# Key loads of the second and third group moved ahead of weight loads in a delta-rule and two-layer feed-forward kernel

## The chip, the cores and the metric

The kernel runs on one core of a Trainium2 chip. The metric is the device time of one execution in microseconds, as the median of several runs.

## What is computed

The reference runs a delta-rule attention over 768 steps and puts two feed-forward layers behind it. All is in fp32. Batch 4, 8 heads, head size 48, so 3072 tokens of width 384; both layers go from 384 to 2048 and back.

```python
k_n = k / (norm(k) + 1e-6)
for t in range(S):
    y[:, :, t] = einsum('bhd,bhde->bhe', q[:, :, t], state)
    v_old = einsum('bhde,bhd->bhe', state, k_n[t])
    state = state + beta[t] * einsum('bhd,bhe->bhde', k_n[t], v[t] - v_old)
x = y as 3072 x 384
h = x @ w_in;   g = h if h >= 1, 0 if h <= -1, else (h + 1)**2 / 4;   x = g @ w_out
h = x @ w_in2;  g = max(h, 0)**2;                                     out = g @ w_out2
```

## The kernel before

The 768 steps are cut into 24 chunks of 32 steps. Four chunks form a group (six groups). For each chunk TensorE makes the products of its keys and queries (`gram`, line 319; for the first group line 354). The dependence between steps inside a chunk needs the inverse of a triangular matrix, and that is done for a whole group at once (`tri`: a transpose on VectorE, small operations for the norms, then 30 pairs of multiply and add, lines 478 and 479, and a transpose back, line 482). The first group's inversion runs on VectorE in two halves that `ld` and `dld` join on TensorE (lines 506 and 514); the inversions of the other groups run on GpSimd. After it each chunk takes its four steps in order, because the state passes from chunk to chunk: ks and yy (line 542), tr (556), sps (591) with its yy (579), and xt (623), the transposes that bring the result into layout for the feed-forward layer.

The first layer then works on blocks of four chunks, 512 tokens. A block has 16 units, one for each 128 columns of the hidden width. Unit f makes hidden product f (nine matmuls into h, 128 x 512, three of them with the low half of x), ScalarE and VectorE make g of it and split it into a high and a low half, and TensorE adds out product f - 2 (nine matmuls into three accumulators `acc`). Each unit has two slots, 2f and 2f + 1, into which other work is put by hand: `put_a` and `put` add a piece at a slot number. In block 0 these are the grams of the third group, the chunk steps of the second group, and the inversion of the third group. In block n are the chunk steps of group n + 1.

Weights arrive as raw halves of 0.39 MB (`load_w`), two to a weight tile, in the order `needed`. Block 0 is also where they are unpacked: two sign-bit passes on ScalarE (`whole_bits`, lines 195 and 196), joined words on VectorE (`make`, line 202), the high half on ScalarE (`upper`, line 232) and the low half on VectorE (`lower`, line 236). Tiles 0 to 2 are made during the first group's chain of steps, the others in units 0 to 12 (`between`): unit f takes up the raw halves of tile f + 3.

All loads go out on SyncE's queue, which takes them in program order. `loads(m, ...)` lets at most m of the loads it lists be under way (`pace`). Keys for a gram come into the ring `kqg` of KG = 2 buffers (`load_kg`), so that a third chunk waits for the gram of the first. Keys for the chunk steps (`load_kq`) and values (`load_kv`) have rings of their own. A few early arrays stand in weight tiles that come into use only later: `spare` and `room`.

On TensorE the order is that of the program. Its first products are the grams of the first two groups, then the first group's chain, then block 0.

Of the kernel before, what the change touches and what calls it, by code (L numbers as in the profile page):

```python
# [8 lines left out]
F32 = mybir.dt.float32  # L9
# [16 lines left out]
def kernel(  # L26
# [23 lines left out]
    NCH, P, DM = out.shape  # L50
    NF = w1.shape[0]
    B, H, T = 4, 8, 32
    D = DM // H
    KT = DM // P
    B2 = B // 2
# [12 lines left out]
    KQ, KG = 3, 2  # L68
# [6 lines left out]
    ring = ctx.enter_context(tc.tile_pool(name="ring", bufs=1))  # L75
# [16 lines left out]
    def weights(x):  # L92
        if x not in both:
            both[x] = wp.tile([P, 2, 2, DM], F32R, tag=f"w{x}", name=f"w{x}")
        return both[x]
# [23 lines left out]
    kqt, kvt, gp, nt, xh, xl = {}, {}, {}, {}, {}, {}  # L119
# [17 lines left out]
    kqg = {}  # L137

    def load_kg(c):
        if c < NCH and c not in kqg:  # L140
            kqg[c] = fetch_kq(c, ring.tile([P, B2, H, 2 * T], F32, tag="kqg", bufs=KG, name="kqt"))

    def fetch_kq(c, t):
        both = [nc.sync.dma_start(
            t[64 * o:64 * o + D].rearrange("p b h x -> p (b h x)"), kq[c, D * o:D * (o + 1)]
        ).ins for o in range(2)]
        pace(*both)
        return t
# [12 lines left out]
    def pace(*ins):  # L161

        m = flight[0]
        if m:
            if len(sent) >= m:
                for x in ins:
                    wait_for(x, sent[-m], "few loads under way")
            sent.append(ins[-1])
# [31 lines left out]
    def joined_words(raw, shape):  # L200
        t = ring.tile(shape, F32, tag="wl", bufs=WL, name="wl")
        nc.vector.scalar_tensor_tensor(
            t.bitcast(I32), raw[..., 1], 3, raw[..., 0],
            ALU.logical_shift_left, ALU.bitwise_or,
        )
        return t
# [14 lines left out]
    def halves(x):  # L221
        return sign_bits(raws[x])

    def whole_bits(x):
        for f in halves(x):
            f()

    def make(x):
        words[x] = joined_words(raws.pop(x), [P, 2, DM])

    def upper(x):
        nc.scalar.copy(weights(x)[:, :, 0], words[x])

    def lower(x):
        t = weights(x)
        nc.vector.tensor_sub(t[:, :, 1], words.pop(x), t[:, :, 0].bitcast(F32))
# [55 lines left out]
    def value(c):  # L292

        g, j = group_of[c]
        return nc.gpsimd.tensor_mul(
            kvt[c][:, 1], kvt[c][:, 1],
            nt[g][:, j * H:(j + 1) * H].rearrange("p (h o) -> p h o", o=1)
            .to_broadcast([P, H, D]),
        )
# [6 lines left out]
    def gram(c, lo=0, hi=2, late=0, eng=None, side=0):  # L306


        n, j = group_of[c]
        if j == 0 and lo == 0:  # L310
            gp[n] = ring.tile([P, 2, GC, H, T], F32, tag="gp", bufs=2, name="gp")
            if GROUPS[n] < GC:
                nc.gpsimd.memset(gp[n][:, 0, GROUPS[n]:], 0.0)
        g = att([P, H, hi - lo, T], "g", side)
        src = kqg[c]

        def one_(b, h, p, pd):
            x = src[pd, b // 2, h]
            nc.tensor.matmul(  # L319
                g[p, h].rearrange("p x i -> p (x i)"), x[:, 0:T], x[:, lo * T:hi * T],  # L320
                start=h == 0, stop=True, skip_group_check=True,
            )

        per_bh(one_)
        kqg.pop(c)
        if late < 2:
            load_kg(c + KG)

        dst = gp[n][:, lo:hi, j].rearrange("p x h i -> p h x i")
        if late > 1:  # L330
            nc.scalar.copy(dst, g)

        def keep():
            (eng or nc.vector).tensor_mul(
                dst,
                dst if late > 1 else g,
                mask[:, lo:hi].rearrange("p (o x) i -> p o x i", o=1)
                .to_broadcast([P, H, hi - lo, T]),
            )

        if late:
            return keep
        keep()
# [22 lines left out]
    def mask_of_head(c):  # L366
# [5 lines left out]
    spare = {  # L372
        "z": (NF - 1, 0), "d": (NF - 1, 1024), "l": (NF - 2, 0), "cross": (NF - 2, 1024),
        "kq": (NF - 3, 0), "u0": (NF - 3, 1024),
    }
    rooms = {}

    def room(name, size):
        x, lo = spare[name]
        if x not in rooms:  # L380
            rooms[x] = wp.tile([P, 4 * DM], F32, tag=f"w{x}", name="room")
        return rooms[x][:, lo:lo + size]
# [398 lines left out]
    NW, NP = 2 * NF, NF  # L781
# [26 lines left out]
    def put(n, slot, *fs):  # L808
        for i, f in enumerate(fs):
            exb.setdefault(SL * n + slot + i, []).append(f)  # L810
# [9 lines left out]
    def put_a(n, slot, *fs):  # L820
        exa.setdefault(SL * n + slot, []).extend(fs)

    def two_grams(c):
        gram(c)
        gram(c + 1, side=1)
# [26 lines left out]
    with tc.manual_schedule():  # L852
# [22 lines left out]
        def loads(m, what):  # L875
            flight[0] = m
            for kind, c in what:
                kind(c)
            flight[0] = 0

        def ws(a, z):
            return [(load_w, needed[x]) for x in range(a, z)]

        def kgs(c):
            return [(load_kg, c)]

        def kvs(c):
            return [(load_kv, c)]

        loads(2, kgs(4) + kgs(5) + ws(0, 1) + kgs(6) + ws(1, 2) + kgs(7) + kvs(0) + ws(2, 3) + kvs(1) + ws(3, 4))  # L890
        loads(1, kvs(2) + ws(4, 5) + kvs(3) + ws(5, 9))
        begin, pre, steps, end = tri(0, V, True)
        begin()
        pre[0]()
# [3 lines left out]
        for c in range(FIRST_GROUP):  # L898
            save0(c)
        masks.append(gram(6, late=2, eng=G))  # L900
        whole_bits(0)
        masks.append(gram(7, late=2, eng=G))
        ins = go(steps)
        rows0()
# [10 lines left out]
        begin1, pre1, steps1, end1 = tri(1, G)  # L915
# [2 lines left out]
                chunk_steps(c) for c in range(FIRST_GROUP)]  # L918
        ld0(0)
        ld0(1)  # L920
        make(0)
        dld0(0)
        dld0(1)
        upper(0)
        s0()
        t0()
        lower(0)
        ld0(2)
        s1()
        ld0(3)  # L930
        t1()
        whole_bits(1)
        begin1()
        k0()
        pre1[0]()
        k1()
        make(1)
        dld0(2)
        go(pre1[1:-2])
        s2()  # L940
        q1()
        t2()
        upper(1)
        go(pre1[-2:])
# [22 lines left out]
        x3()  # L967
        x0()
        k3()
        loads(2, ws(9, 12) + [(load_kq, 4)] + ws(12, 13) + [(load_kq, 5)] + ws(13, 16) + kgs(8) + ws(16, 18) + kgs(9))  # L970
        loads(2, ws(18, NW))
        turn[0] = None

        put(0, 12, end1)
        put(0, 11, lambda: value(4))
        put(0, 12, lambda: value(5))
        put(0, 14, lambda: value(6))
        put(0, 21, lambda: value(7))
        for c, at_ in ((4, (13, 15, 17, 18)), (5, (19, 20, 21, 22)),
                       (6, (23, 24, 25, 26)), (7, (27, 28, 29, 30))):  # L980
            def steps_of(c=c, box={}):
                if c not in box:
                    box[c] = chunk_steps(c)
                return box[c]
            for i, slot in enumerate(at_):
                put_a(0, slot, lambda i=i, g=steps_of: g()[i]())
        put(0, SL - 1, lambda: first2(RAW))

        at, ready = {}, {}
        for c, slot in ((8, 8), (10, 10)):  # L990
            ready[c + 1] = slot
            put_a(0, slot, lambda c=c: two_grams(c))
        for n in range(2, NB):
            todo = []
            for j, c in enumerate(range(FIRST[n], FIRST[n] + SIZES[n])):
                if n < NB - 1 and 2 * j < SIZES[n + 1]:
                    x = FIRST[n + 1] + 2 * j
# [3 lines left out]
            for i, (mark, s_) in enumerate(todo):  # L1001
                slot = SL * (n - 1) + i * SL // len(todo)
# [95 lines left out]
```

## Time and profile before

| | us |
|---|---|
| median of 3 runs (lowest to highest) | 1055.08 (1054.01 to 1056.84) |
| the profiled execution | 1058.46 |
| its span, first to last instruction | 1056.7 |
| TensorE busy | 988.0 (93%) |
| VectorE / ScalarE / GpSimd busy | 518.2 / 433.9 / 297.1 |
| mean granted TensorE clock, of full speed | 0.976 |

How to read it: the span is cut into stretches, and for each the profile has the busy time of every engine, the clock that TensorE was granted, as a share of full speed, and what the DMA engines moved. Full speed is 2.4 GHz, the lower level 1.2 GHz; a share in between means that both levels occur in the stretch. TensorE's idle time is then put down to what ended it. SyncE has no work of its own; its rows are the moments at which loads are sent. A load lands some us later, and the chain of waits shows from when to when.

### The profile page before, as it was taken

The page shows a single profiled execution, that of the slowest core. Times are in us where ns is not written, and L with a number is a line of the kernel's source. Part 1 is how long each engine was busy: PE and PEld are TensorE (multiplying, and loading weights), DVE is VectorE, ACT ScalarE, POOL GpSimd, SP SyncE. Part 2 cuts the span into 40 slices and gives each one's busy share as a digit, 9 for nine tenths or more (in the row PEclk, how much of TensorE's full clock was granted, in tenths as well). Part 3 has the DMA queues.
Part 4 walks back from the last instruction along what each step waited for, and adds up shares of the span by engine and source line. Part 5 has one row for each costly group of instructions (what it writes and reads, how often), then busy time and mean ns, then how long its engine had stood idle before and what let it go on. Part 6 is the DMA issues. An engine that isn't in the chain of part 4 may idle for free.

```text
span 1056.7 us, 29989 instructions
## 1 busy us (share of the span) xinstructions
PE 988.0 (93%) x13416; PEld 838.0 (79%) x13416; DVE 518.2 (49%) x801; ACT 433.9 (41%) x745; POOL 297.1 (28%) x414
## 2 busy tenths in 40 slices
PE   5787387899999999999999999999999999999998
PEld 4675266678888777888888888998989999999997
DVE  4437246657555655765544666544333343333333
ACT  2237135435544453554554554333323333333322
POOL 1478005922950780395110112111020020100000
PEclk9998678899999999999999999999999999999999
DMA  6437731144334434334333114101010000000000
GB/s 139 140 91 210 210 75 33 49 135 108 99 117 135 120 101 115 98 87 150 107 100 99 60 60 128 37 1 60 1 53 8 1 30 1 1 30 1 31 1 30
DMA packets 33937, 80.68 MB, mean 76 GB/s; under 512 B 4368, under 2 KB 11664, under 8 KB 33808
## 3 DMA queue, kind: packets, MB, share of 16 engines
q1 hardware_dynamic: 33808, 78.76, 25.5%
q8 instruction: 105, 1.72, 0.7%
q14 instruction: 24, 0.20, 0.1%
HBM read 63.01 MB, written 15.73 MB: 75 GB/s over the span
## 4 chain that ended last, share of the span: by engine, by line
PE 82%; DMA 8%; DVE 5%; ACT 2%; issue 2%; SPq 0%; POOL 0%; ACTq 0%; DVEq 0%; POOLq 0%
PE h L638 35%; PE acc L638 35%; DMA raw<-in_w_dram 4%; DMA kqt<-in_kq_dram 2%; PE tr L556 2%; PE yy L579 2%; PE sps L591 2%; PE yy L542 2%; PE ks L542 1%; DVE gp L482 1%; PE g L319 1%; PE xt L623 1%; DMA room<-in_kq_dram 1%; DVE gm L418 1%; ACT r L670 1%
## 5 line engine op out<-in xcount | busy, mean ns | idle before, releaser
L638 PE MATMUL acc<-w,gg 128*128 128x384 f32 x1152 | 217.3, 337 | 1.7 <-ACT e L697 1.7
L638 PE MATMUL h<-x2s,w 128*128 128x512 f32 x864 | 214.6, 392 | 0.0
L638 PEld LDWEIGHTS acc<-w,gg 128*128 128x128 f32 x1152 | 203.9, 187 | 10.0 <-ACT e L697 2.3
L638 PEld LDWEIGHTS h<-x2s,w 128*128 128x128 f32 x864 | 160.8, 188 | 29.3
L638 PE MATMUL h<-xh,w 128*128 128x512 f32 x576 | 155.1, 405 | 4.8 <-ACT r L670 4.8
L638 PE MATMUL acc<-gh,w 128*128 128x512 f32 x576 | 157.3, 409 | 0.8 <-ACT gh L687 0.8
L678 DVE TENSOR_TENSOR rg<-rg 128x512 f32<-128x512 f32 x96 | 69.6, 725 | 143.4 <-ACT rg L677 143.4
L638 PEld LDWEIGHTS h<-xh,w 128*128 128x128 f32 x576 | 107.8, 192 | 29.4 <-ACT r L670 5.3
L638 PEld LDWEIGHTS acc<-gh,w 128*128 128x128 f32 x576 | 105.9, 192 | 24.6 <-ACT gh L687 1.2
L677 ACT ACTIVATE rg<-h,zero 128x512 f32<-128x512 f32 x96 | 66.2, 689 | 138.4 <-PE h L638 138.4
L689 DVE TENSOR_TENSOR gg<-rg,gg 128x512 fp32r<-128x512 f32 x96 | 67.2, 700 | 104.0 <-ACT gg L687 104.0
L670 ACT ACTIVATE r<-h,one 128x512 f32<-128x512 f32 x96 | 66.0, 687 | 124.1 <-PE h L638 123.6
L687 ACT CAST gg<-rg 128x512 fp32r<-128x512 f32 x96 | 59.7, 622 | 118.3 <-PE acc L638 114.2
L687 ACT CAST gh<-g 128x512 fp32r<-128x512 f32 x96 | 59.5, 620 | 117.5 <-DVE g L674 72.3
L689 DVE TENSOR_TENSOR gl<-g,gh 128x512 fp32r<-128x512 f32 x96 | 74.7, 778 | 62.0 <-ACT gh L687 43.1
L479 POOL TENSOR_TENSOR tx<-tx,t 128x30 f32<-128x30 f32 (+9 forms) x150 | 100.7, 671 | 11.5
L671 DVE TENSOR_SCALAR g<-r 128x512 f32<-128x512 f32 x96 | 47.7, 497 | 112.0 <-ACT r L670 111.5
L478 POOL TENSOR_TENSOR t<-tx,gm 128x30 f32<-128x30 f32 (+9 forms) x150 | 93.3, 622 | 13.4 <-DVE tx L457 2.2
L674 DVE SCALAR_TENSOR_TENSOR g<-r,g 128x512 f32<-128x512 f32 x96 | 76.7, 799 | 35.2 <-ACT g L673 35.2
L638 PE MATMUL acc<-gl,w 128*128 128x512 f32 x288 | 83.3, 398 | 0.0
L638 PE MATMUL h<-xl,w 128*128 128x512 f32 x288 | 83.0, 397 | 0.1
L673 ACT ACTIVATE g<-g 128x512 f32<-128x512 f32 x96 | 60.4, 629 | 33.1 <-DVE g L671 31.6
(117 smaller groups left out, 902.1 us busy)
## 6 DMA issues: line engine op xcount, KB each, us to landing
raw<-in_w_dram SPq DMA_DIRECT2D x64, 384.0 KB, 3.5
kqt<-in_kq_dram SPq DMA_DIRECT2D x86, 192.0 KB, 4.0
kv<-in_kv_dram SPq DMA_DIRECT2D x24, 384.0 KB, 3.5
w2f<-wl SPq DMA_DIRECT2D x32, 192.0 KB, 3.9
w2r<-w2f SPq DMA_DIRECT2D x16, 384.0 KB, 3.1
x<-e SPq DMA_DIRECT2D x18, 256.0 KB, 2.3
x2r<-x SPq DMA_DIRECT2D x6, 768.0 KB, 4.9
out_dram<-e SPq DMA_DIRECT2D x23, 192.0 KB, 2.0
```

The lines of the kernel that those rows point to most:

```text
L478: eng.tensor_mul(t, by.to_broadcast(shape), of.to_broadcast(shape))
L479: return eng.tensor_add(rest, rest, t)
L542: per_bh(lambda b, h, p, pd: nc.tensor.matmul(o[p, h], kqt[c][pd, b // 2, h, x * T:(x + 1) * T], st[pd, b // 2, h], start=h == 0, stop=x = ...
L638: nc.tensor.matmul(o, *((r, l) if swap else (l, r)), **flags)
L670: marks[0] = nc.scalar.activation(r, h, AF.Relu, bias=one)
L671: marks[1] = nc.vector.tensor_scalar(g, r, 2.0, 0.5, ALU.min, ALU.mult)
L673: nc.scalar.activation(g, g, AF.Square)
L674: nc.vector.scalar_tensor_tensor(g, r, -1.0, g, ALU.add, ALU.max)
L677: marks[0] = nc.scalar.activation(r, h, AF.Relu, bias=zero)
L678: marks[1] = nc.vector.tensor_mul(g, r, r)
L687: nc.scalar.copy(ghi, g)
L689: nc.vector.tensor_sub(glo, g, ghi.bitcast(F32))
```

## The change

- Key chunks 6 and 7 of the second group no longer go through the ring `kqg`: they have places of their own in weight tiles 12 and 11 (`spare`), so that all four of the group's loads are sent one behind the other, ahead of any weight.
- During the first group's chain 14 raw weight halves are loaded, the last ten of them one at a time, in place of nine, the last five one at a time.
- After the chain come four halves, the keys of chunks 4 and 5 for their steps, the keys of chunks 8 and 9 for their grams, and four more halves. The last ten halves are sent from slot 9, behind the keys of chunks 10 and 11, which the grams of 8 and 9 ask for.
- Unpacking of tiles 0 and 1 stands later among the chain's steps.
- Slots: the end of the second group's inversion 12 to 11; steps of chunks 4, 5 and 6 one to three slots earlier; the grams of chunks 10 and 11 from slot 10 to 11.

```diff
     def load_kg(c):
         if c < NCH and c not in kqg:
-            kqg[c] = fetch_kq(c, ring.tile([P, B2, H, 2 * T], F32, tag="kqg", bufs=KG, name="kqt"))
+            if f"kg{c}" in spare:
+                t = room(f"kg{c}", B2 * H * 2 * T).rearrange("p (b h x) -> p b h x", b=B2, h=H)
+            else:
+                t = ring.tile([P, B2, H, 2 * T], F32, tag="kqg", bufs=KG, name="kqt")
+            kqg[c] = fetch_kq(c, t)
...
         "kq": (NF - 3, 0), "u0": (NF - 3, 1024),
+        "kg6": (NF - 4, 0), "kg7": (NF - 5, 0),
     }
...
-        loads(2, kgs(4) + kgs(5) + ws(0, 1) + kgs(6) + ws(1, 2) + kgs(7) + kvs(0) + ws(2, 3) + kvs(1) + ws(3, 4))
-        loads(1, kvs(2) + ws(4, 5) + kvs(3) + ws(5, 9))
+        loads(2, [(load_kg, c) for c in range(4, 8)] + kvs(0) + kvs(1) + ws(0, 4))
+        loads(1, kvs(2) + kvs(3) + ws(4, 14))
...
         masks.append(gram(6, late=2, eng=G))
-        whole_bits(0)
         masks.append(gram(7, late=2, eng=G))
...
         ld0(1)
-        make(0)
         dld0(0)
         dld0(1)
-        upper(0)
+        whole_bits(0)
         s0()
         t0()
-        lower(0)
+        make(0)
         ld0(2)
         s1()
+        upper(0)
         ld0(3)
         t1()
+        lower(0)
...
         k1()
-        make(1)
         dld0(2)
         go(pre1[1:-2])
         s2()
         q1()
+        make(1)
         t2()
...
-        loads(2, ws(9, 12) + [(load_kq, 4)] + ws(12, 13) + [(load_kq, 5)] + ws(13, 16) + kgs(8) + ws(16, 18) + kgs(9))
-        loads(2, ws(18, NW))
+        loads(2, ws(14, 18) + [(load_kq, 4), (load_kq, 5)] + kgs(8) + kgs(9) + ws(18, 22))
...
-        put(0, 12, end1)
+        put(0, 9, lambda: loads(2, ws(22, NW)))
+        put(0, 11, end1)
...
-        for c, at_ in ((4, (13, 15, 17, 18)), (5, (19, 20, 21, 22)),
-                       (6, (23, 24, 25, 26)), (7, (27, 28, 29, 30))):
+        for c, at_ in ((4, (12, 13, 14, 15)), (5, (17, 18, 19, 20)),
+                       (6, (22, 23, 24, 25)), (7, (27, 28, 29, 30))):
...
-        for c, slot in ((8, 8), (10, 10)):
+        for c, slot in ((8, 8), (10, 11)):
```

SyncE's queue from the end of the chain's weight loads to the third group's keys, before. `raw` is a weight half, `kqt` half of a chunk's keys (two loads for a chunk), `kv` a chunk's keys and values in token layout; the first `kqt` row is chunk 6, the next ones are 4, 5, 8, 9, and the last row begins with 10 and 11.

```order
L186 DMA raw<-in_w_dram 128x768 x4
L144 DMA kqt<-in_kq_dram 48x1024 x2
L155 DMA kv<-in_kv_dram 128x768 x3
L186 DMA raw<-in_w_dram 128x768 x3
L144 DMA kqt<-in_kq_dram 48x1024 x2
L186 DMA raw<-in_w_dram 128x768
L144 DMA kqt<-in_kq_dram 48x1024 x2
L186 DMA raw<-in_w_dram 128x768 x3
L144 DMA kqt<-in_kq_dram 48x1024 x2
L186 DMA raw<-in_w_dram 128x768 x2
L144 DMA kqt<-in_kq_dram 48x1024 x2
L186 DMA raw<-in_w_dram 128x768 x14
```

The same stretch after: the row of eight holds chunks 4, 5, 8 and 9, the row of four chunks 10 and 11.

```order
L190 DMA raw<-in_w_dram 128x768 x10
L148 DMA kqt<-in_kq_dram 48x1024 x2
L159 DMA kv<-in_kv_dram 128x768 x3
L190 DMA raw<-in_w_dram 128x768 x4
L148 DMA kqt<-in_kq_dram 48x1024 x8
L190 DMA raw<-in_w_dram 128x768 x4
L148 DMA kqt<-in_kq_dram 48x1024 x4
L190 DMA raw<-in_w_dram 128x768 x10
```

The keys of chunks 10 and 11 stood behind the 14 last halves; now ten halves stand behind the keys.

TensorE in block 0, before: unit 5's hidden product, the grams of chunks 10 and 11 (one row of 64), out product 3, hidden product 6.

```order
L638 MATMUL h<-xl,w_1696 128x512 x3
L319 MATMUL g<-kqt 32x64 x64
L638 MATMUL acc_1708<-gh,w_1696 128x512 x2
L638 MATMUL acc_1709<-gh,w_1696 128x512 x2
L638 MATMUL acc_1710<-gh,w_1696 128x512 x2
L638 MATMUL acc_1708<-gl,w_1696 128x512
L638 MATMUL acc_1709<-gl,w_1696 128x512
L638 MATMUL acc_1710<-gl,w_1696 128x512
L638 MATMUL h<-xh,w_1735 128x512 x6
```

After, from the same hidden product on:

```order
L643 MATMUL h<-xl,w_1681 128x512 x3
L643 MATMUL acc_1693<-gh,w_1681 128x512 x2
L643 MATMUL acc_1694<-gh,w_1681 128x512 x2
L643 MATMUL acc_1695<-gh,w_1681 128x512 x2
L643 MATMUL acc_1693<-gl,w_1681 128x512
L643 MATMUL acc_1694<-gl,w_1681 128x512
L643 MATMUL acc_1695<-gl,w_1681 128x512
L323 MATMUL g<-kqt 32x64 x64
L643 MATMUL h<-xh,w_1720 128x512 x6
L643 MATMUL h<-xl,w_1720 128x512 x3
L547 MATMUL ks<-st,kqt 32x48 x32
L547 MATMUL yy<-st,kqt 32x48 x32
```

Out product 3 goes ahead of the two grams, and ks and yy of chunk 4 stand right behind hidden product 6.

## Rows read from the trace of the kernel before

**Rows 1.** Stretches: length; busy (instructions) per engine; clock; DMA share; GB/s

```profile
97.90:143.40 45.50, 21.70 (x293) 17.00 (x294) 13.99 (x18) 11.32 (x17) 5.23 (x7) 0.62 0.69 190
143.40:221.70 78.30, 67.96 (x1473) 53.14 (x1471) 50.28 (x70) 42.06 (x69) 45.25 (x65) 0.91 0.15 40
221.70:400.00 178.30, 177.76 (x3658) 143.13 (x3658) 108.91 (x173) 86.49 (x161) 89.00 (x132) 1.00 0.42 121
400.00:1056.70 656.70, 650.38 (x5691) 564.80 (x5689) 298.57 (x450) 258.66 (x436) 104.08 (x120) 1.00 0.16 51
```

**Rows 2.** The chain of waits from 79 us: start, length, what

```profile
79.36 4.99 DMA raw<-in_w_dram
...
102.32 4.05 DMA kqt<-in_kq_dram
...
130.11 5.80 DMA kqt<-in_kq_dram
...
183.50 2.29 PE h L638 x9
```

**Rows 3.** Timeline of SyncE's queue: start, first to last issue, what, count

```profile
37.58 0.33 SPq L155 DMA_DIRECT2D kv<-in_kv_dram  x1
...
47.87 10.82 SPq L186 DMA_DIRECT2D raw<-in_w_dram  x4
...
104.97 24.62 SPq L186 DMA_DIRECT2D raw<-in_w_dram  x14
129.63 20.34 SPq L144 DMA_DIRECT2D kqt<-in_kq_dram  x10
```

**Rows 4.** Timeline of TensorE in block 0: start, length, what [idle before, releaser]

```profile
97.86 2.93 PE L638 MATMUL h<-xh,w 128*128 128x512 f32 x6 [4.41 <-ACT r L670]
...
105.73 0.42 PE L319 MATMUL g<-kqt 48*32 48x64 f32 x2 [2.58 <-DMA kqt<-in_kq_dram]
...
108.27 2.93 PE L638 MATMUL acc<-gh,w 128*128 128x512 f32 x6
...
112.27 1.64 PE L638 MATMUL h<-xh,w 128*128 128x512 f32 x6
...
135.26 0.39 PE L319 MATMUL g<-kqt 48*32 48x64 f32 x2 [20.66 <-DMA kqt<-in_kq_dram]
...
143.36 1.53 PE L638 MATMUL h<-xh,w 128*128 128x512 f32 x6
```

**Rows 5.** TensorE's waits from 143.36 to 221.72 (total, times, longest); next block's start

```profile
PE yy L542 <- DVE xl L626: 6.5, 3, 2.5
PE xt L623 <- ACT kv L607: 2.7, 1, 2.7
...
221.72 1.67 PE L638 MATMUL h<-xh,w 128*128 128x512 f32 x6
```

**Rows 6.** Timeline in the first group's chain: VectorE, TensorE twice, ScalarE

```profile
28.63 1.05 DVE L502 STREAM_TRANSPOSE room<-tx 128x512 f32<-128x512 f32 x1
...
33.11 1.90 PE L506 MATMUL z<-room 32*32 32x16 f32 x128
...
40.43 0.93 PE L556 MATMUL tr<-kv,gp 32*32 32x48 f32 x34 [1.46 <-issue]
...
64.73 0.91 ACT L195 ACTIVATE raw<-raw 128x768 f32<-128x768 f32 x1
```

**Rows 7.** Timeline around the third group's inversion on GpSimd: VectorE and GpSimd

```profile
148.98 0.95 DVE L236 TENSOR_TENSOR w<-wl,w 128x768 fp32r<-128x768 f32 x1
...
168.12 1.28 POOL L448 TENSOR_TENSOR gm<-gm,st 128x256 f32<-128x256 f32 x1 [64.75 <-DVE st L437]
...
181.98 1.58 DVE L236 TENSOR_TENSOR w<-wl,w 128x768 fp32r<-128x768 f32 x1
...
216.51 0.62 POOL L479 TENSOR_TENSOR tx<-tx,t 128x30 f32<-128x30 f32 x1
...
225.23 2.18 DVE L482 STREAM_TRANSPOSE gp<-tx 128x1024 f32<-128x1024 f32 x1
```

## The prediction

> **What bounds the kernel now.** I read the 40 slices first, then the table by stretch, then the chain of waits and the timelines of SyncE and TensorE in the stretch that stood out. From 221.7 us on TensorE is busy in 177.76 of 178.30 us and then in 650.38 of 656.70 us, at a granted clock of 1.00 [rows 1]. That part is a block of TensorE work, the change leaves its matmuls alone, and it moves as a whole: whatever is won or lost must happen before the second block of layer one starts its first product at 221.72 [rows 5]. Before that, two stretches are poor. In 97.9 to 143.4 TensorE is busy 21.70 of 45.50 us at a clock of 0.62; in 143.4 to 221.7 it is busy 67.96 of 78.30 at 0.91 [rows 1].
>
> The first is a wait for a load. The chain that ended last runs through DMAs from 79.36 to 135.91 [rows 2], and TensorE stands still for 20.66 us before the scores (the key products, "grams") of chunk 10, with the keys named as releaser [rows 4]. Behind that gram, in program order, stand out product 3 and hidden product 6, so all of block 0 waits. Why the keys are late is seen on SyncE's queue: after 104.97 it sends 14 weight halves, 24.62 us of them, and only at 129.63 the keys of chunk 10 [rows 3]. None of those 14 halves was what TensorE needed next; the weights of unit 5 had been there. The second stretch has another cause: waits of 6.5 us for VectorE's xl (three yy products share a PSUM buffer with the transposes just ahead of them) and of 2.7 us for ScalarE [rows 5], most of its 10.34 idle us.
>
> **The change, part by part.**
>
> A. Key chunks 6 and 7 get places in weight tiles 12 and 11. Before, gram 7 stood on TensorE in front of the first inverse product (z, line 506), which began at 33.11 although its last input, VectorE's transpose, was done at 28.63 + 1.05 = 29.68 [rows 6]. With all four key chunks under way first, gram 7 ends before that, and z can start 3.4 us earlier. What follows, up to the chain's end at 79.36 [rows 2], is a chain of short dependent products, so it should shift as a whole. Against it: ten weight halves (before, five) are now loaded beside the chain, one at a time. TensorE has gaps there in which it waits for nothing the profile shows, 1.46 us at 40.43 where loads run [rows 6]. In the chain's second half, which before had hardly any load beside it, I allow for three such gaps of some 1 us. So A is between 0 and 3.4; I take **2.5 us**, since at most part of the gaps can grow. The moved conversions (make, upper and lower of tile 0 and 1) go behind chain work on VectorE and ScalarE, so they cost the chain nothing; their cover is that the first hidden product comes 40 us later.
>
> B. From the end of the chain to hidden product 6. Before, 79.36 to 143.36, 64.0 us. After, step by step from the chain's end. Hidden 4 starts when ScalarE has let go of the buffer h, not when a load lands [rows 4]: 97.86 - 79.36 = 18.5 us, unchanged. From its start to the end of the two grams 8 and 9 it was 108.27 - 97.86 = 10.4, of which 2.6 was a wait for keys [rows 4]: 7.8 without it, so 26.3. Out 2 took 112.27 - 108.27 = 4.0, at half clock [rows 4]: 30.3. Hidden 5, nine matmuls at full clock, 2.29 us as at 183.50 [rows 2]: 32.6. Grams 10 and 11 and out 3 took 143.36 - 135.26 = 8.1 at half clock [rows 4], half of that at full clock, 4.1: hidden 6 at 36.7 to 40.7. I take **39**, against 64.0: a gain of **25 us**.
>
> That needs the keys in time. Load rate: between 79.36 and 106.37 thirteen loads landed (nine weight halves, four key chunks; the queue below the diff counts them), 2.08 us each [rows 2]; the fourteen halves after it took 1.76 each [rows 3]. After the change eight loads bring the keys of 9: 16.6 us. In front of them may still lie what the queue held back: the one-at-a-time loads are 3.5 us apart [rows 3]; if they begin at about 37, as before at 37.58 [rows 3], the twelve end at about 79, as late as the chain, and the keys of chunk 6 and two of three value loads (the queue rows below the diff) stand behind them, some 6 us. So keys 9 land 17 to 23 us after the chain's end and gram 9 wants them at about 24. Keys 10 go out when gram 8 has ended and four more halves have been issued, 21 to 27, and land 4 to 6 us later (before: 5.8 [rows 2]), 25 to 33, against a need at 35 (hidden 5's end and out 3). It fits with a margin of 2 us at the late end. If both are late, B loses up to 5: its range is 20 to 27. The ten halves that now stand behind keys 10 and 11 on SyncE's queue go out from 27 on, 1.76 each, all there by 46; the last is asked for in unit 12, after 75. That is free.
>
> The Trainium skill (DMA: Bandwidth & Descriptors, Anatomy of one DMA) prices a single DMA at about 2.0 us plus its bytes over 436 GB/s, for these 0.39 MB an estimate of 2.9 us; the rows above say 3.5. By the page the twelve loads would end at about 72 and rival 1 would be less likely; by the rows they end with the chain. I go by the rows.
>
> C. From hidden 6 to the first product of the next block: 221.72 - 143.36 = 78.4 us. The slots of chunks 5 to 7 now leave half a unit or more between a transpose and the yy product that shares its buffer, so the 6.5 us go, and the 2.7 us at least in part. In their place chunks 4 and 6 now have only one product of 2.3 us between ks and tr, where VectorE must subtract in between: perhaps 1 us for each. VectorE is still loaded by the start of the third group's inversion in units 7 to 9. If nothing were idle it would be 68 us at the same clock. I take **70**, a gain of **8**, with 1 (the stalls only change their name) and 11 (no idle, full clock) as ends.
>
> D. What is late next: the inversion of group 3 on GpSimd. It ran from 168.12 to 217.1, 49 us, and VectorE's transpose of its result began at 225.23 [rows 7], 8 us later. Its start is tied to unit 9, its end to a slot in unit 16; those come some 14 us nearer to each other. So VectorE will wait about 5 us for GpSimd there; TensorE has some 12 us of products (hidden 16 and 17, a pair of grams, two outs, ks) ahead of the first tr that needs the result. I take a cost of **1 us**, 0 to 4.
>
> The sum: 2.5 + 25 + 8 - 1 = **34.5 us**. Against the profiled execution (1058.46 us, span 1056.7) that is 1024; the runs' median, 1055.08, lies 3.4 us below the profiled one, and taken off the median it gives 1020.6, so **1021 us**. The ends add up to 17 and 41.4; both sets of ends at once are unlikely.
>
> **The rivals.**
>
> 1. The keys of 8 to 11 are still late, since the one-at-a-time loads run past the chain and hold back everything behind them. For it: the estimate above ends at the same moment as the chain. Against: only 8 loads are then left before keys 9, not 13. Price: about 8 us of wait in place of the 20.66. Time 1029.
>
> 2. GpSimd's inversion of group 3 becomes the wait at the border of the blocks. For it: VectorE and GpSimd slow each other where both work; the same subtraction (line 236) took 0.95 us at 148.98 with GpSimd idle and 1.58 at 181.98 with it busy [rows 7], and block 0 is packed more densely now. Price: 5 us on the inversion, with 5 more that the 12 us of cover no longer take: gain 26, time 1029. The Trainium skill (GPSIMD Engine Reference, Key points) says that GpSimd shares its SBUF interfaces with VectorE and contends with instructions that have two SBUF inputs; the trace agrees with the two rows just named.
>
> 3. The second half of block 0 doesn't shrink: ScalarE and VectorE were its bound and the waits only move to h and tr. C is 0 to 1: time 1028.
>
> 4. Slower than before. ScalarE takes its instructions in order, and the sign bits of weight tile 2 stand in its queue inside the chain, between the copies that the chain needs. Its halves are now behind two value loads sent one at a time. By 3.5 us a load they land at about 51; before, ScalarE took them up at 64.73 [rows 6], so the need is at about 61. For a loss the four loads would have to last over 58 us instead of 14, 14.5 us each. At 16 us each the chain would end 40 us late, 5 us more than is won: time 1060. Nothing in the trace is near that.
>
> 5. The change doesn't do what it says: something else on SyncE's queue or TensorE's order holds unit 5 until the weights are all there. Within 0.3%, time 1055.
>
> **How the numbers follow.** The forecast 1021 has 0.58; rival 1 0.14, rival 2 0.10, rival 3 0.12, rival 4 0.03, rival 5 0.03. The first four cases are all faster by over 0.3% (3 us, about what a measurement of this kernel can tell from no change): 0.94; same 0.03; slower 0.03. The range takes in the forecast with its bounds and the rivals at 1028 and 1029: 1013 to 1034.
>
> **What would show it.** Right: no wait over 3 us for keys before the grams of chunks 10 and 11, and hidden 6 within 41 us of the chain's end; z at about 30; the yy waits for xl gone; the next block's first product at about 187; TensorE busy as before from there. Wrong: a key wait of 5 us or more (rival 1, step B's loads), VectorE's transpose of group 3's result waiting for GpSimd with TensorE idle behind it (rival 2), idle time in units 6 to 15 still near 10 us (rival 3), or a chain that ends after 79.7 (step A).

## The result, and the profile after

| us | before | after |
|---|---|---|
| median (lowest to highest) | 1055.03 (1054.01 to 1056.84) | 1023.45 (1021.05 to 1027.41) |
| ratio to before, 95% interval | | 0.970 (0.966 to 0.974) |
| the profiled execution, its span | 1058.46, 1056.7 | 1027.41, 1025.7 |
| A: first hidden product starts | 79.70 | 79.37 |
| B: from it to hidden product 6 | 63.66 | 38.46 |
| C: hidden product 6 to the next block's first product | 78.36 | 74.44 |
| the rest of the span | 834.98 | 833.43 |

The changed kernel is faster by 3%; the forecast was 1021. The stages are read at three starts that every timeline of TensorE shows. Their gains are 0.3, 25.2, 3.9 and 1.6, together 31.0 us of span. A and C fell short of the forecast, and the rest, for which a cost of 1 us was forecast, came out better. The prediction counts the chain's end from a load that goes out at 79.36; the table counts it from the first hidden product, at 79.70.

The same stretches as [rows 1], after (columns: length; busy and instructions of TensorE, its weight loads, VectorE, ScalarE, GpSimd; granted clock; DMA share; GB/s):

```profile
97.30:117.80 20.50, 16.72 (x292) 12.99 (x292) 14.63 (x19) 11.89 (x17) 5.26 (x7) 0.83 0.76 199
117.80:192.30 74.50, 66.42 (x1476) 52.34 (x1473) 48.87 (x69) 42.04 (x68) 42.20 (x58) 0.93 0.34 94
192.30:400.00 207.70, 205.80 (x4202) 165.95 (x4202) 124.74 (x196) 99.32 (x183) 94.10 (x141) 1.00 0.39 116
400.00:1025.70 625.70, 621.75 (x5147) 542.26 (x5145) 283.78 (x427) 245.99 (x415) 102.58 (x119) 1.00 0.16 50
```

The first stretch has the same work as before in 20.5 in place of 45.5 us, at a clock of 0.83 in place of 0.62. The second is shorter by only 3.8 us, and TensorE is still idle for 8.1 of its 74.5 us.

SyncE's queue after, beside [rows 3] (start, first to last issue, what, count):

```profile
45.65 34.57 SPq L190 DMA_DIRECT2D raw<-in_w_dram  x10
...
82.63 9.00 SPq L190 DMA_DIRECT2D raw<-in_w_dram  x4
93.26 6.52 SPq L148 DMA_DIRECT2D kqt<-in_kq_dram  x8
101.41 7.19 SPq L190 DMA_DIRECT2D raw<-in_w_dram  x4
108.72 2.04 SPq L148 DMA_DIRECT2D kqt<-in_kq_dram  x4
110.81 17.92 SPq L190 DMA_DIRECT2D raw<-in_w_dram  x10
```

The keys of chunks 10 and 11 go out at 108.72, 20.9 us earlier than before. The last of the ten loads sent one at a time goes out at 45.65 + 34.57 = 80.22, behind the chain's end at 79.37.

TensorE's timeline after, beside [rows 4] (start, length, what [idle before, releaser]):

```profile
103.39 1.09 PE L323 MATMUL g<-kqt 48*32 48x64 f32 x62 [0.66 <-DMA kqt<-in_kq_dram]
...
112.79 0.27 PE L323 MATMUL g<-kqt 48*32 48x64 f32 x2 [1.91 <-DMA kqt<-in_kq_dram]
113.69 1.31 PE L323 MATMUL g<-kqt 48*32 48x64 f32 x62 [0.63 <-DMA kqt<-in_kq_dram]
115.17 0.39 PE L323 MATMUL g<-kqt 48*32 48x64 f32 x2 [0.17 <-DMA kqt<-in_kq_dram]
115.97 1.92 PE L323 MATMUL g<-kqt 48*32 48x64 f32 x62 [0.41 <-DMA kqt<-in_kq_dram]
117.83 2.93 PE L643 MATMUL h<-xh,w 128*128 128x512 f32 x6
```

The one wait of 20.66 us is now four of 3.1 us together before the grams of 10 and 11. In the stretch after hidden product 6 the waits for xl of [rows 5] are gone, and others are there:

```profile
126.63 0.88 PE L561 MATMUL tr<-kv,gp 32*32 32x48 f32 x64 [1.12 <-DVE kv L557]
...
145.68 1.50 PE L561 MATMUL tr<-kv,gp 32*32 32x48 f32 x64 [3.36 <-DVE kv L557]
...
167.08 0.88 PE L561 MATMUL tr<-kv,gp 32*32 32x48 f32 x64 [3.01 <-DVE kv L557]
...
182.88 0.88 PE L561 MATMUL tr<-kv,gp 32*32 32x48 f32 x64 [0.44 <-DVE kv L557]
```

### The profile page after: what moved, and what is told of

Same layout as the page of the kernel before. It is cut to its first block, busy times and chain, and to the rows that moved or that the text cites. A ratio compares the mean times of both kernels' runs of the same rounds, so it can differ in the third digit from the quotient of the medians.

```text
span 1025.7 us, 29990 instructions
## 1 busy us (share of the span) xinstructions
PE 979.7 (96%) x13416; PEld 832.9 (81%) x13416; DVE 518.7 (51%) x801; ACT 434.5 (42%) x745; POOL 296.5 (29%) x414
## 4 chain that ended last, share of the span: by engine, by line
PE 79%; DMA 10%; POOL 4%; DVE 3%; issue 2%; ACT 1%; SPq 1%; POOLq 0%; ACTq 0%; DVEq 0%
PE h L643 36%; PE acc L643 36%; DMA raw<-in_w_dram 6%; DMA kqt<-in_kq_dram 2%; POOL tx L484 2%; POOL t L483 2%; PE tr L561 1%; PE yy L584 1%; PE sps L596 1%; DMA room<-in_kq_dram 1%; DMA kv<-in_kv_dram 1%; PE yy L547 1%; PE ks L547 1%; DVE gp L487 1%; PE g L323 1%
## 5 line engine op out<-in xcount | busy, mean ns | idle before, releaser
L643 PEld LDWEIGHTS h<-x2s,w 128*128 128x128 f32 x864 | 161.0, 188 | 29.2
L643 PE MATMUL acc<-gh,w 128*128 128x512 f32 x576 | 155.1, 405 | 0.5 <-ACT gh L692 0.5
L694 DVE TENSOR_TENSOR gl<-g,gh 128x512 fp32r<-128x512 f32 x96 | 74.5, 776 | 54.0 <-ACT gh L692 42.6
```

Source lines behind the costliest of these rows:

```text
L643: nc.tensor.matmul(o, *((r, l) if swap else (l, r)), **flags)
L694: nc.vector.tensor_sub(glo, g, ghi.bitcast(F32))
```

## The experiments

All times are medians of each kernel's runs beside runs of the kernel before on the same chip; where there is no ratio, it is one time. A, B and C are the stages of the table above, from each kernel's own profile.

| kernel | us | ratio (95%) | A | B | C |
|---|---|---|---|---|---|
| order alone (from before) | 1031.09 | 0.979 (0.975 to 0.982) | 78.87 | 38.08 | 78.94 |
| weights ahead of keys 10, 11 | 1041.55 | 0.989 (0.986 to 0.991) | 78.10 | 53.15 | 75.02 |
| old slots of chunks 4 to 6 | 1028.77 | 0.976 (0.972 to 0.980) | 77.63 | 35.12 | 78.06 |
| tr half a unit later | 1023.99 | 0.972 (0.968 to 0.977) | 76.87 | 39.58 | 72.88 |
| nine halves in the chain | 1026.18 | | 76.81 | 37.64 | 74.96 |
| six halves in the chain | 1027.08 | | 78.92 | 37.33 | 76.49 |
| places undone | 1025.43 | | 79.52 | 33.27 | 76.17 |
| keys first | 1020.56 | | 75.98 | 35.68 | 75.79 |
| keys first, again | 1022.04 | 0.968 (0.966 to 0.970) | 78.86 | 32.11 | 76.23 |
| the changed kernel, again | 1023.79 | 0.970 (0.967 to 0.973) | 78.11 | 34.44 | 73.62 |
| chunk 4 earlier, 6 later | 1024.52 | 0.970 (0.968 to 0.973) | 78.13 | 36.50 | 76.75 |
| inversion's start spread | 1020.88 | 0.968 (0.965 to 0.970) | 77.93 | 35.55 | 76.44 |

The changed kernel's two profiles differ by 1.3, 4.0 and 0.8 us in A, B and C. Less than that between two kernels is read here only from the waits by name, or from several profiles. Some parts of the change were not undone by themselves, the later unpacking of tiles 0 and 1 and the new slot for the end of the second group's inversion among them.

**Is the order on the queue the gain of B, or the five more halves that are there early?** Two kernels take one of the two each. The first is the kernel before with its last 14 halves behind the keys of 10 and 11 and nothing else:

```diff
-        loads(2, ws(18, NW))
+        put(0, 9, lambda: loads(2, ws(18, NW)))
```

> The kernel before with one edit: its last 14 weight halves are sent from slot 9, behind the keys of chunks 10 and 11. Nothing is loaded earlier, the chain and the slots are as before. Theory (the order on SyncE's queue was the price): the 20.66 us wait for the keys of chunk 10 shrinks to under 6 us, hidden product 6 starts at about 122 instead of 143.4, and the time is about 1034 (gain 21). Rival (too few weights had been loaded; the keys only hid it): units 6 to 12 then wait for the halves that now go later, hidden product 6 comes earlier but the next block starts at 215 or later, and the time is 1048 or more.

The second is the changed kernel with its last ten halves ahead of those keys again:

```diff
-        put(0, 9, lambda: loads(2, ws(22, NW)))
+        loads(2, ws(22, NW))
```

> The changed kernel with its last ten weight halves sent right behind the four before them, ahead of the keys of chunks 10 and 11, as in the kernel before. Theory: the ten halves at 1.76 to 2.08 us put the keys 18 to 21 us later; they land at 130 to 136 instead of 115, so that the wait before grams 10 and 11 comes back with about 15 us and the time is about 1039. Rival (the 14 halves loaded during the chain were the gain, the order is worth little): within 5 us of the changed kernel, under 1029.

The queue of the second kernel, and TensorE before its gram of chunk 10:

```profile
97.09 23.91 SPq L190 DMA_DIRECT2D raw<-in_w_dram  x14
121.04 16.20 SPq L148 DMA_DIRECT2D kqt<-in_kq_dram  x10
```

```profile
127.02 0.39 PE L323 MATMUL g<-kqt 48*32 48x64 f32 x2 [18.48 <-DMA kqt<-in_kq_dram]
```

The wait is back with 18.48 us, with 14 halves loaded in the chain. B is 53.15 there, 10.5 less than before: fewer halves stand between the chain and the keys, so the same wait starts and ends earlier. With the order alone B is 38.08, a gain of 25.6 us, which is as much as the whole change has (25.2), and grams 10 and 11 run without a wait:

```profile
112.85 1.99 PE L319 MATMUL g<-kqt 48*32 48x64 f32 x128
```

So the order is enough for the 25 us of B. In time it brings 22 us: 1031.09, where the kernel before took 1053.12 beside it. Whether the early halves add to B is not settled: five profiles of kernels that have the changed kernel's loads behind the chain (the changed kernel twice, old slots, tr later, places undone) show 33.27 to 39.58, against 38.08 in one profile of the order alone.

**Does C's gain come from the slots?** The changed kernel with the old slots, and with tr of chunks 5 and 6 half a unit later:

```diff
-        for c, at_ in ((4, (12, 13, 14, 15)), (5, (17, 18, 19, 20)),
-                       (6, (22, 23, 24, 25)), (7, (27, 28, 29, 30))):
+        for c, at_ in ((4, (13, 15, 17, 18)), (5, (19, 20, 21, 22)),
+                       (6, (23, 24, 25, 26)), (7, (27, 28, 29, 30))):
```

> The changed kernel with the chunk steps of chunks 4 to 6 in the slots of the kernel before. Theory (the new slots removed the waits of yy for xl, 6.5 us before, but put waits of tr for VectorE in their place, 7.9 us in the changed kernel): the stretch from hidden product 6 to the next block takes 74 to 78 us, 0 to 4 more than the 74.4 of the changed kernel; time 1023 to 1028. Rival (the slots gave nothing, all of that stretch's gain comes from the rest): same or faster, 1020 to 1023.

```diff
-        for c, at_ in ((4, (12, 13, 14, 15)), (5, (17, 18, 19, 20)),
-                       (6, (22, 23, 24, 25)), (7, (27, 28, 29, 30))):
+        for c, at_ in ((4, (12, 13, 14, 15)), (5, (17, 19, 20, 21)),
+                       (6, (22, 24, 25, 26)), (7, (27, 28, 29, 30))):
```

> The changed kernel with tr, sps and xt of chunks 5 and 6 one slot later each, which puts an out or hidden product (2.3 us) more between ks and tr. Theory (tr waits 3.36 and 3.01 us for VectorE's subtraction, and the lower clock after them costs some 3 more): the waits fall to about 1 us each, the stretch to 69 to 71 us, and the time to about 1019. Rival (VectorE and ScalarE are the bound in units 8 to 12): the wait moves on to sps, xt or the next yy and the time stays within 1 us.

TensorE's waits in stage C with the old slots (engine, operation and line, waited for: us in total, times, longest):

```profile
PE yy L547 <- DVE xl L631: 6.5, 3, 2.5
PE xt L628 <- ACT kv L612: 2.7, 1, 2.7
```

and with tr half a unit later:

```profile
PE sps L596 <- ACT kv L572: 3.2, 1, 3.2
PE tr L561 <- DVE kv L557: 2.4, 2, 1.3
PE yy L547 <- DVE xl L631: 1.6, 1, 1.6
```

With the old slots the two waits of [rows 5] are there again to the tenth of a us, and C is 78.06, as in the kernel before (78.36) and in the one with the order alone (78.94). Eight profiles with the changed kernel's slots have 73.62 to 76.49, 75.3 on average, against 78.5 for these three. So the slots of the steps bring C's gain, some 3 us. With tr half a unit later the 7.9 us of waits at tr shrink to 2.4, but ScalarE's copy behind tr is now late for sps (3.2) and one wait for xl returns (1.6). C is 72.88, not the expected 69 to 71, and the time of 1023.99 is that of the changed kernel, as the rival had it. A wait that is moved by one slot changes its name.

**Does loading beside the chain lengthen TensorE's stops in it?** Fewer halves in the chain, the rest behind it:

```diff
-        loads(1, kvs(2) + kvs(3) + ws(4, 14))
+        loads(1, kvs(2) + kvs(3) + ws(4, 9))
...
-        loads(2, ws(14, 18) + [(load_kq, 4), (load_kq, 5)] + kgs(8) + kgs(9) + ws(18, 22))
+        loads(2, ws(9, 14) + kgs(8) + kgs(9) + ws(14, 18) + [(load_kq, 4), (load_kq, 5)] + ws(18, 20))
...
-        put(0, 9, lambda: loads(2, ws(22, NW)))
+        put(0, 9, lambda: loads(2, ws(20, NW)))
```

> The changed kernel with 9 instead of 14 weight halves loaded during the chain; the other five go out right behind it, then the keys of 8 and 9. Theory (loads beside the chain lengthen the time TensorE waits for its own next instructions, which come in 16 KB packets over the same DMA engines): from the first such wait to the last the chain took 32.0 and 32.5 us with 9 halves and 33.1 to 34.5 with 14 in the runs so far; here 32 to 32.6, all of them less where no load runs (after about 62 us), and the chain ends at 76.5 to 77.5. Rival (the waits have nothing to do with the loads and differ by chance): 33 to 34.5 as in the runs with 14.

The second goes further, with `ws(4, 6)` in the first line, `ws(6, 13) + kgs(8) + kgs(9) + ws(13, 16) + [(load_kq, 4), (load_kq, 5)] + ws(16, 18)` in the second and `ws(18, NW)` at slot 9.

> The changed kernel with 6 instead of 14 weight halves loaded during the chain, eight behind it, the keys of 8 and 9 after seven of them. Theory: loads end at about 52, so the waits for instructions after 55 are at most 0.7 us each, the stretch between the first and the last of them takes 31 to 32 us and the chain ends at about 76. What it costs: units 1 to 4 take up weights that land 2 us apart from the chain's end on, so hidden product 6 comes 40 to 44 us after the chain. Rival (chance): the stretch takes 33 to 34.5.

TensorE in the chain with six halves:

```profile
33.80 1.52 PE L519 MATMUL w<-gp,room 32*32 32x16 f32 x99 [1.48 <-issue]
35.11 0.27 PE L561 MATMUL tr<-kv,gp 32*32 32x48 f32 x2
35.16 0.21 PE L519 MATMUL w<-gp,room 32*32 32x16 f32 x1
35.16 0.78 PE L561 MATMUL tr<-kv,gp 32*32 32x48 f32 x26
39.32 0.93 PE L561 MATMUL tr<-kv,gp 32*32 32x48 f32 x34 [3.38 <-issue]
```

Stops "for issue" are waits for nothing that the profile shows. The longest of any run, 3.38 us, is in the kernel with the fewest loads. From the first stop to the last it takes 35.0 us here, 33.6 with nine halves and 33.1 to 34.5 in the kernels with 14 and the places for chunks 6 and 7, against 32.0 before and 32.5 with the order alone. The expected 31 to 32.6 was missed twice, in one profile each: the theory that the weight loads lengthen these stops is not borne out. The nine halves' chain ended at 76.81, as expected; with six it ended at 78.92, not 76, and hidden product 6 came 37.33 us after it, not 40 to 44.

**What are the places for chunks 6 and 7 worth?** The changed kernel without them:

```diff
-        "kg6": (NF - 4, 0), "kg7": (NF - 5, 0),
...
-        loads(2, [(load_kg, c) for c in range(4, 8)] + kvs(0) + kvs(1) + ws(0, 4))
+        loads(2, kgs(4) + kgs(5) + ws(0, 1) + kgs(6) + ws(1, 2) + kgs(7) + kvs(0) + ws(2, 3) + kvs(1) + ws(3, 4))
```

> The changed kernel with key chunks 6 and 7 back in the ring and in the loading order of before; all else is as changed. Theory (the places bring the first inverse product 3.3 us forward, but TensorE's instruction stream takes most of it back): the first inverse product at 32 to 33, the end of the chain 0.5 to 1.5 us later than in the runs with places (76.9 to 79.4). Rival (the shift goes through whole, as the prediction had it): the chain ends 3 us later, at 80 to 82.

z starts at 31.68 there and the first hidden product at 79.52. Over all profiles z starts at 29.3 on average with the places (27.50 to 29.90) and at 32.2 in the three without them, and the first hidden product at 77.9 (75.98 to 79.37, eleven profiles) against 79.4 (78.87 to 79.70, three). So the places bring z forward by 2.9 us, and about 1.5 us of that is left at the chain's end. TensorE's stops take up the rest: they add up to 7.2 to 8.3 us in the three kernels without the places, one of which loads 14 halves beside the chain, and to 8.9 to 10.3 in the eleven with them.

**Are the keys of 10 and 11 better sent directly behind those of 9?** The four halves between them go behind:

```diff
-        loads(2, ws(14, 18) + [(load_kq, 4), (load_kq, 5)] + kgs(8) + kgs(9) + ws(18, 22))
+        loads(2, ws(14, 18) + [(load_kq, 4), (load_kq, 5)] + kgs(8) + kgs(9))
...
-        put(0, 9, lambda: loads(2, ws(22, NW)))
+        put(0, 9, lambda: loads(2, ws(18, NW)))
```

> The changed kernel with the four halves that stand between the keys of 9 and those of 10 moved behind the keys of 11. Theory (what is left of the wait for keys, 3.1 us in the changed kernel, is these four loads on SyncE's queue): the keys of 10 go out when gram 8 ends, the waits before grams 10 and 11 fall under 1 us together, and hidden product 6 comes 35 to 37 us after the chain, not 38.5. Rival (the keys' own landing time is the rest): 38 or more.

> The changed kernel with the four halves between the keys of 9 and of 10 moved behind the keys of 11, now timed. Theory: hidden product 6 comes about 3 us sooner after the chain than in the changed kernel (35.7 in the one look), ratio 0.965 to 0.970. Rival (the one look was a lucky chain): the ratio of the changed kernel, 0.970 to 0.974.

Beside the second of these ran the changed kernel again:

> The changed kernel itself, on the chip and in the rounds of the next three. Theory (the end of the chain moves by 1 to 2 us from run to run with the landing of the first loads, the rest of the gain is steady): ratio to the kernel before 0.968 to 0.974, chain end between 76 and 79.5 us, hidden product 6 38 to 40 us after it, next block 73 to 76 us after that.

SyncE's queue and TensorE's grams with the keys first, in the second of the two:

```profile
89.22 14.92 SPq L148 DMA_DIRECT2D kqt<-in_kq_dram  x12
104.19 26.31 SPq L190 DMA_DIRECT2D raw<-in_w_dram  x14
```

```profile
109.05 1.99 PE L323 MATMUL g<-kqt 48*32 48x64 f32 x128
```

No gram of 10 or 11 waits for its keys in either profile (B 35.68 and 32.11). In the repeat of the changed kernel TensorE's only wait for keys in B is one of 0.89 us, and B is 34.44, not the 38 to 40 expected. With the medians 1022.04 and 1023.79 and intervals that overlap, the kernel with the keys first is not shown to be faster.

Five profiles have the changed kernel's loads behind the first group's chain. In them the wait goes with how late the last of the one-at-a-time loads is sent, seen from the chain's end; no run changed that by itself. In order: 2.9 us ahead of it (places undone) all waits for keys in B are 0.4 us; 2.1 and 1.9 ahead (old slots; the repeat) 0.9 and 0.9; 0.9 and 1.4 behind (the first profile; tr later) 3.8 and 3.4.

**Can the waits at tr be removed?** Two kernels start from keys first. One puts the steps of chunk 4 a slot earlier and those of chunk 6 a slot later (with `value(4)` at slot 9 and the second pair of grams at slot 10 again), so that ks and tr lie otherwise to the units' own work:

```diff
-        for c, at_ in ((4, (12, 13, 14, 15)), (5, (17, 18, 19, 20)),
-                       (6, (22, 23, 24, 25)), (7, (27, 28, 29, 30))):
+        for c, at_ in ((4, (11, 12, 13, 14)), (5, (17, 18, 19, 20)),
+                       (6, (23, 24, 25, 26)), (7, (27, 28, 29, 30))):
```

> The kernel of e9 with the steps of chunk 4 one slot earlier (11 to 14, values of chunk 4 at slot 9, grams 10 and 11 at slot 10) and those of chunk 6 one slot later (23 to 26). Theory (ks in an odd slot has VectorE's subtraction in front of the next unit's work, in an even slot behind it; that is why tr of chunks 4 and 6 waits 1.1 to 1.9 and 3.0 us): both waits go, one yy wait of 1.6 us for xl comes back before chunk 7, and the stretch from hidden product 6 takes 72 to 74 us. Rival: VectorE is the bound, the waits move on and the stretch stays at 75 to 76.

```profile
PE tr L561 <- DVE kv L557: 7.6, 2, 4.1
...
ACT st L287 <- DVE gm L423: 3.3, 1, 3.3
```

The other also spreads the start of the third group's inversion, which puts that wait of ScalarE into the same units:

```diff
-                put(0, a + i // 3, s_)
+                put(0, a + 1 + i // 3, s_)
...
-            a = max(a, 13)
+            a = max(a, 12)
```

> The kernel of e10 with the transpose that begins the third group's inversion one slot earlier and the square root that needs it as before, so that a whole unit lies between them (all later groups: the small operations one slot later). Theory (tr of chunk 5 waits 3.8 us because ScalarE stands 2.9 us in front of that square root, waiting for the transpose): the wait of ScalarE goes, the one of tr falls under 2 us, and the stretch takes 69 to 71 us, ratio 0.962 to 0.967. Rival: the rest of the inversion's start on VectorE is the cause, and nothing changes by over 1 us.

```profile
PE tr L561 <- DVE kv L557: 5.7, 2, 3.6
PE yy L584 <- issue: 1.9, 1, 1.9
...
PE sps L596 <- ACT kv L572: 1.1, 1, 1.1
```

In the first the wait at chunk 4 goes (1.83 us with keys first), that at chunk 6, which should have gone too, stays (3.44 after 3.08), and C is 76.75, outside the 72 to 74 expected: that the slots' place against the units alone makes these waits is not borne out. In the second ScalarE's wait for gm is gone and the sum at tr is down by 1.9 us, but C stays at 76.44 (69 to 71 expected): a wait of 1.1 us at sps and a stop for "issue" of 1.9 stand there instead. Its ratio, 0.968, is not shown to differ from that of keys first. What is taken from one wait comes back at the next, or as such a stop.

## Why the prediction was right, and where it was off

**B, the mechanism right, the number in part luck: 25 forecast, 25.2 measured, 29.2 in the repeat.** The wait was for an order on a queue and not for a rate, and the order alone removes it. The forecast 39 from the chain's end to hidden product 6 stands against 38.46. Two errors cancel in it. The keys were late: those of chunk 10 landed some 34 us after the chain's end and those of chunk 11 just before the gram at 115.97, 36.6 after it, and not 25 to 33, since the one-at-a-time loads went out 34.57 / 9 = 3.8 us apart, not 3.5, and ended 0.9 us behind the chain; the four halves ahead of those keys took 7.2 us. That is rival 1 in small, 3.1 us of wait at the grams of 10 and 11 in place of its 8. And TensorE was there early, at 112.79 - 1.91 = 110.88, 31.5 us after the chain's end in place of 35. The term for out 2 is half of that. It was taken over from [rows 4] with 4.0 us, at half clock (granted 0.50, the lower level), where it followed a wait of 2.58 us for keys; after, it follows one of 0.66 us, is granted 1.00 and takes 106.59 - 104.41 = 2.2:

```profile
104.41 1.66 PE L643 MATMUL acc<-gh,w 128*128 128x512 f32 x6
...
106.59 1.54 PE L643 MATMUL h<-xh,w 128*128 128x512 f32 x6
```

So a wait that goes takes some of the half clock behind it along, which the prediction counted only from hidden product 5 on. With out 2 at full clock the sum's low end of 36.7 would have been some 35. The repeat, with hardly a wait for keys, has 34.44, a gain of 29.2 us, which is past the 27 that the prediction set as B's upper end.

The Trainium skill (DMA: Bandwidth & Descriptors, Anatomy of one DMA) was set against the rows here, with an estimate of 2.9 us for such a load. That section gives its figures for loads that GpSimd issues, and these go out on SyncE's queue, so the estimate is not one for them. The measured 3.8 us decides for the rows.

**C, the term that was mis-sized: 8 forecast, 3.9 measured.** The 9.2 us of waits that [rows 5] show went, as forecast. In their place the prediction allowed 1 us each at tr of chunks 4 and 6. It was 1.12 and 3.01 there, and 3.36 and 0.44 at chunks 5 and 7, 7.9 us in all. The step that failed is the one that looked at the number of TensorE products between ks and tr. Chunk 5 has one there as before, and its wait is the longest; before, one of yy's waits for xl, 2.4 us, had stood between its ks and tr. What decides is VectorE's and ScalarE's own queue at that moment. VectorE ahead of the longest of the waits:

```profile
136.00 2.19 DVE L423 STREAM_TRANSPOSE gm<-gp 128x1024 f32<-128x1024 f32 x1
...
141.25 0.69 DVE L679 SCALAR_TENSOR_TENSOR g<-r,g 128x512 f32<-128x512 f32 x1 [1.65 <-ACT g L678]
...
145.08 0.55 DVE L557 TENSOR_TENSOR kv<-kv,ks 128x384 f32<-128x384 f32 x1
```

The subtraction that tr waits for is 0.55 us long and starts at 145.08, behind the transpose for the third group's inversion, a unit's own product and the making of a weight tile; VectorE itself waits 1.65 us for ScalarE in between. So rival 3 (the second half doesn't shrink, the waits only move) describes half of what happened. Of the 3.9 us, TensorE's busy time gave 67.96 - 66.42 = 1.5, with the clock at 0.93 in place of 0.91, and its idle time 10.3 - 8.1 = 2.3. That VectorE and ScalarE together bound units 8 to 12 is what the last two experiments fit with; it is not shown by one that takes work off them. The prediction's upper end of 11 for C is not "no idle, full clock" as it says: no idle time at the clock of before already gives 78.4 - 68 = 10.4, and at full clock 67.96 x 0.91 = 62 us would be left, an estimate, a gain of 16.

**A, mis-sized: 2.5 forecast, 0.3 between the first two profiles, 1.5 over fourteen.** z started at 29.83, as forecast for about 30, and what it waits for is VectorE's transpose:

```profile
29.83 1.90 PE L511 MATMUL z<-room 32*32 32x16 f32 x128 [1.49 <-DVE room L507]
```

The mechanism by which the shift was then to be kept, a chain that moves as a whole, failed in part. TensorE's stops for "issue" between 29 and 80 us, before, and then after (the two largest groups each):

```profile
PE tr L556 <- issue: 3.1, 4, 1.5
PE w L514 <- issue: 1.4, 1, 1.4
```

```profile
PE tr L561 <- issue: 4.2, 4, 1.7
PE w L519 <- issue: 2.0, 1, 2.0
```

With three smaller groups each (1.0, 0.9 and 0.8 before; 1.7, 1.2 and 1.0 after) they add up to 7.2 us before and to 10.1 after. That the stops would grow where loads run beside them was the prediction's reason for 2.5 instead of 3.4. The two kernels with fewer loads speak against that reason, and so does the one without the places, whose stops add up to 8.3 us beside all 14 halves. What makes them longer where z starts earlier stays open.

**D, about right: 1 forecast, 0.8 of waits, and rival 2 not seen.** GpSimd's inversion of the third group, VectorE's transpose of it, and TensorE's next ks and yy:

```profile
196.19 0.26 POOL L484 TENSOR_TENSOR tx<-tx,t 128x30 f32<-128x30 f32 x1
...
196.49 2.23 DVE L487 STREAM_TRANSPOSE gp<-tx 128x1024 f32<-128x1024 f32 x1 [0.48 <-POOL tx L484]
198.59 0.67 DVE L338 TENSOR_TENSOR gp<-g,mask 128x512 f32<-128x512 f32 x1
...
199.31 0.88 PE L547 MATMUL ks<-st,kqt 48*32 48x48 f32 x64 [0.50 <-DVE gp L338]
...
200.51 0.88 PE L547 MATMUL yy<-st,kqt 48*32 48x48 f32 x64 [0.32 <-DVE gp L338]
```

The 8 us of margin in [rows 7] are used up, as forecast, but VectorE waited 0.48 us and not 5, and no product of TensorE waits for that transpose itself. Ks and yy wait 0.8 us for what VectorE does right behind it. The rest of the span is 1.6 us shorter all the same: the waits of out products for ScalarE (e) fell from 1.7 us to 0.2. That is read from one profile each, and the rest takes 831.5 to 835.5 us in the profiles of all kernels here, so it is no gain that the change is shown to bring.

**Rivals 4 and 5** (slower, no change) did not come: ScalarE took up the sign bits of tile 2 at 63.87 (64.73 before), and the chain did not end later than before in any profile. The median is 2.5 us above the forecast; of the sum's 34.5 us, C lacks 4.1, A 2.2, and the rest of the span (D) gave 2.6 more.

## What to carry to other kernels

Where an engine waits for a load, look first at what stands ahead of that load on its queue and when each of those is needed: here fourteen loads that nobody asked for soon stood ahead of the keys of two chunks that everything waited for, and moving them behind, one line, brought 22 us of time, where the whole change brought 32. Where loads are sent one at a time beside other work, compare the end of that row with the moment at which the next urgent load is due; in five profiles the wait that was left went with one to four microseconds there. A wait in a stretch where three engines are all loaded is not worth its length: of 9.2 us of waits removed, 3.9 us of time were gained.

## What the runs showed of the hardware

**TensorE stops every 256 instructions in the chain of small products.** In the rows with six halves above, 99 + 2 + 1 + 26 = 128 matmuls lie between two stops, each with a weight load of its own. The stops are 3.3 to 4.4 us apart in most cases. In the whole run the profile counts these packets:

```profile
q8 instruction: 105, 1.72, 0.7%
```

That is 16.4 KB each. The Trainium skill (Runtime: NRT & Kernel Launch, Instruction fetch mechanics) says that an engine's instructions are refilled in blocks of 16 KiB, 256 instructions, by the sequencer's own DMA queue; the count between two stops and the size of the packets agree. The page calls the fetch hidden; here it is not in this stretch, if that is what the stops are: they take 7 to 10 of 51 us. No run here changed the number of instructions, so it is not shown that the fetch makes them.

**VectorE beside GpSimd.** The subtraction of [rows 7], which took 0.95 us with GpSimd idle, in the profile after, while the inversion runs:

```profile
165.22 1.34 DVE L240 TENSOR_TENSOR w<-wl,w 128x768 fp32r<-128x768 f32 x1
```

It takes 1.34 us there. The Trainium skill (GPSIMD Engine Reference, Key points) says that GpSimd contends with VectorE's instructions that have two SBUF inputs; the trace agrees. The denser block 0 did not make it worse than the 1.58 of before.
